# Linear attention with a gated feed-forward block: w3 and w_out loaded and folded first, constants on VectorE, and a newly searched order of steps, loads and queues

## The chip, the cores and the metric

The kernel runs on one core of a Trainium2 chip. The metric is the device time of one execution in microseconds (us). The kernel before takes 258.12 us, the median of three runs (257.49 to 262.9).

Every ratio below is the mean time of one kernel's fast runs over the mean time of the other's fast runs of the same rounds, so it is not quite the ratio of the medians that stand beside it. On one core a run is called slow when it is over 1.5% above the fastest of the same kernel; the others are called fast. Intervals are 95% intervals.

## The reference

There are 8 batches, 8 heads, 576 positions and heads of 64. After the attention the heads of a position are laid side by side, which gives 4608 tokens of 512.

```python
def phi(x):
    return np.where(x > 0, x, np.exp(x) - 1.0) + 1.0
q_p, k_p = phi(q), phi(k)
kv  = np.einsum('bhsd,bhse->bhde', k_p, v)
z   = np.sum(k_p, axis=2)
num = np.einsum('bhsd,bhde->bhse', q_p, kv)
den = np.einsum('bhsd,bhd->bhs', q_p, z)[..., None] + 1e-06
x   = (num / den)          # transposed and reshaped to [4608, 512]
a, b = x @ w1, x @ w2      # [4608, 1024] each
out = ((a * b) @ w3) @ w_out
```

Nothing stands between w3 and w_out, so the kernel multiplies these two matrices once (the fold, `wf = w3 @ w_out`) and uses the product.

## The kernel before

The kernel is a set of small steps and a string of tokens. The string fixes the order in which the steps are written, and so the order of the instructions on each engine: in the traces below every engine and every DMA queue works in that order (ScalarE's copy of 0.39 us that has to wait behind two exponentials is an example). A load that waits for a free buffer holds up everything behind it in its queue.

The tokens that matter here are these. L, M and N load k, q and v of a batch (`.0` and `.1` are halves, `.2` the whole, `.3` the remainder of 64 positions); with a `+` the load goes into GpSimd's queue, without it into SyncE's. X, Y and Z are the exponential, minimum and maximum of q, and x, y and z those of k. T transposes q by a DMA in SyncE's queue, and A forms the products that need it. v copies v to bf16, K forms kv, F is one unit of the two wide products (eight matmuls), O an output product and S its store. E, C and B load w3, w_out and w1 with w2. w and W are the transposes and products of the fold, H runs filler matmuls, and I sets constants.

```python
ld  = ctx.enter_context(tc.tile_pool(name="ld", bufs=5))    # q, k, v: five buffers for all
att = ctx.enter_context(tc.tile_pool(name="att", bufs=2))
...
def load_qkv(name, src, b, part, alt=False):
    ...
    return (nc.gpsimd if alt else nc.sync).dma_start(...)   # "+" picks the queue

def v_unit(b, i, alt=False):                                # token v
    ...
    else:                                                   # v.2, the remainder
        copy_of(alt)(out=vr[:, :, 0:D], in_=raw["vr", b]...)  # VectorE with "+", else ScalarE

def qt_load(b, part):                                       # token T
    qj, qr = ph["q", b]
    ...
    nc.sync.dma_start(out=dst, in_=src, transpose=True)

def nat_units(b, js):                                       # token A: nd <- kv, qt
    ...
    nc.tensor.matmul(nd[...], w[rows], kvs[b][rows, hp, u, :], start=True, stop=True)

def f_unit(c, f):                                           # token F: 8 matmuls, 1.73 us
    a_ps, b_ps = f_open(c, f)
    for ps, w in ((a_ps, w1_sb), (b_ps, w2_sb)):
        for kc in range(KC):
            f_mm(c, f, ps, w, kc)
    f_close(c, f, a_ps, b_ps)                               # ScalarE copies a, VectorE multiplies
...
GATES = "B0<L0.1 C0<N0.1 E4<N0.1 M1.2<C1"                   # load on the left waits for the right
for s in ORDER.split():
    step(s)
```

## Time and profile before

| what | value | where it is from |
|---|---|---|
| time | 258.12 us | median of three runs |
| PE busy | 235.0 us, 92% of the span | first line of the page |
| first useful matmul | 14.79 us | timeline of PE |
| first output product | 58.20 us | timeline of PE |
| from there to the end | 196.7 us | 254.9 us of span less 58.20 |
| longest PE wait after that | 0.9 us, on a transposed q | timeline of PE |

PE is the limit from about 25 us on. Before that, loads and PE compete for being it. The following lines are SyncE's entries in the timeline of the kernel before (start of issue, length of issue, queue, what); they are the transpositions of q of batches 2, 3 and 4.

```profile
66.59 3.31 SPq L242 DMA_TRANSPOSE qt<-qj  x1
...
88.47 1.64 SPq L242 DMA_TRANSPOSE qt<-qj  x1
...
104.55 4.78 SPq L242 DMA_TRANSPOSE qt<-qj  x1
```

PE uses the three results from 76.7, 97.8 and 121.9 us on. They are asked for 10, 9 and 17 us ahead, and they land 8.7, 6.0 and 8.3 us after they are asked for. So the first two have 1 to 3 us to spare, and the third has 9.

### The profile page before, as it was taken

To read this page: it belongs to the slowest core of one execution; us is meant where nothing else is said; L and a number is where in the kernel's file an instruction comes from. 1 tells how busy PE (TensorE), PEld (TensorE's weight loads), DVE (VectorE), ACT (ScalarE), POOL (GpSimd) and SP (SyncE) were. 2 spreads that over 40 slices of the span, in tenths; PEclk is the share of its full clock that TensorE was granted. 3 is DMA by queue.
4 is the path that set the end of the run, shared out by engine and by line. 5 is a ranking of instruction groups with operands and counts; after the bars stand their busy time and mean duration, and the time that the engine had idled before them with its cause. 6 is when DMAs were issued, how large, how long until landed. Compare 5 with 4: busy or idle time off the path is not lost.

```text
span 254.9 us, 4477 instructions
## 1 busy us (share of the span) xinstructions
PE 235.0 (92%) x1641; PEld 114.3 (45%) x1660; DVE 166.9 (65%) x425; ACT 130.4 (51%) x206; POOL 42.7 (17%) x69
## 2 busy tenths in 40 slices
PE   0568999999899999999999999989999999999994
PEld 0134444645454554445445444534454444444442
DVE  0586665659779999897992798668856543333230
ACT  3569526968884674675448337534342213323201
POOL 8784185466100010010000000000000000000000
PEclk9999999999999999999999999999999999999999
DMA  5999999999999999959968946983470331200225
GB/s 186 363 254 202 211 287 231 327 260 337 256 322 219 265 254 280 257 140 255 352 175 221 373 84 165 249 217 24 146 215 3 61 115 53 82 0 0 84 85 165
DMA packets 58726, 49.52 MB, mean 194 GB/s; under 512 B 34448, under 2 KB 49040, under 8 KB 58704
## 3 DMA queue, kind: packets, MB, share of 16 engines
q1 hardware_dynamic: 47344, 26.81, 42.1%
...
q14 instruction: 9, 0.07, 0.2%
q10 hardware_dynamic: 144, 0.13, 0.1%
...
## 4 chain that ended last, share of the span: by engine, by line
PE 74%; DMA 17%; POOL 3%; DVE 2%; issue 1%; ACT 1%; ACTq 0%; SPq 0%; DVEq 0%; POOLq 0%
PE b_ps L371 22%; PE a_ps L371 22%; PE o_ps L390 19%; DMA w_sb<-in_moe_w_dram 4%; PE wf_ps L464 4%; DMA qt<-qj 4%; DMA w3b<-in_moe_w_dram 3%; DMA q32r<-in_q_dram 3%; PE kvp L199 3%; DMA k<-in_k_dram 3%; PE nd L265 2%; PE w3p L454 1%; POOL k L120 1%; PE xtp L285 1%; PE o_ps L417 1%
## 5 line engine op out<-in xcount | busy, mean ns | idle before, releaser
L371 PEld LDWEIGHTS <-w_sb 128*128 128x128 bf16 x576 | 54.5, 98 | 66.5 <-DMA w_sb<-in_moe_w_dram 2.1
L377 DVE TENSOR_TENSOR ab<-a_sb,b_ps 128x512 bf16<-128x512 f32 x72 | 49.2, 685 | 50.7 <-PE b_ps L371 46.5
L371 PE MATMUL b_ps<-xt,w_sb 128*128 128x512 bf16 x288 | 74.9, 379 | 1.2 <-ACT o_sb L393 0.7
L371 PE MATMUL a_ps<-xt,w_sb 128*128 128x512 bf16 x288 | 75.1, 380 | 0.3 <-DMA w_sb<-in_moe_w_dram 0.2
L376 ACT COPY a_sb<-a_ps 128x512 f32<-128x512 f32 x72 | 42.1, 586 | 58.1 <-PE a_ps L371 58.1
L390 PE MATMUL o_ps<-wf_sb,ab 128*128 128x512 bf16 x266 | 63.0, 379 | 0.7
L390 PEld LDWEIGHTS <-ab 128*128 128x128 bf16 x280 | 26.8, 98 | 30.9
L393 ACT COPY o_sb<-o_ps 128x512 f32<-128x512 f32 x22 | 12.8, 585 | 38.5 <-PE o_ps L390 38.4
L162 DVE SCALAR_TENSOR_TENSOR qj<-q,e 128x256 bf16<-128x256 f32 x64 | 23.8, 417 | 0.1
L162 DVE SCALAR_TENSOR_TENSOR kj<-k,e 128x256 bf16<-128x256 f32 x64 | 23.7, 416 | 0.0
L141 DVE TENSOR_SCALAR e<-e 128x1024 bf16<-128x1024 bf16 x32 | 13.7, 430 | 12.6 <-ACT e L137 12.6
L137 ACT ACTIVATE e<-q 128x1024 bf16<-128x1024 f32 x16 | 16.9, 1061 | 6.2 <-DMA q<-in_q_dram 6.2
L137 ACT ACTIVATE e<-k 128x1024 bf16<-128x1024 f32 x16 | 16.8, 1056 | 3.1 <-DMA k<-in_k_dram 2.9
L275 DVE TENSOR_TENSOR xn<-nd,r 128x512 bf16<-128x512 f32 x28 | 18.0, 686 | 0.0
L120 POOL DMA_DIRECT2D v<-in_v_dram x7 | 6.1, 869 | 66.3 <-ACT vt L171 44.1
L464 PE MATMUL wf_ps<-wo_sb,w3t 128*128 128x512 bf16 x60 | 14.6, 379 | 0.3 <-issue 0.2
L100 PE MATMUL warm<-zero 128*128 128x512 bf16 x12 | 4.5, 551 | 9.5 <-DVE zero L94 9.5
L171 ACT CAST vt<-v 128x1024 bf16<-128x1024 f32 x12 | 12.6, 1047 | 0.1
L393 DVE COPY o_sb<-o_ps 128x512 f32<-128x512 f32 x13 | 8.9, 686 | 4.4 <-PE o_ps L390 4.4
L120 POOL DMA_DIRECT2D q<-in_q_dram x7 | 6.1, 875 | 33.3 <-ACT a_sb L376 23.6
L464 PEld LDWEIGHTS <-w3t 128*128 128x128 bf16 x64 | 5.9, 98 | 6.3
L199 PE MATMUL kvp<-vt,kj 64*128 64x130 bf16 x224 | 8.7, 217 | 0.0
...
## 6 DMA issues: line engine op xcount, KB each, us to landing
...
```

The source lines that it names most:

```text
L120: return (nc.gpsimd if alt else nc.sync).dma_start(out=t[:, h0 * W:h1 * W].rearrange("p (h x) -> p h x", x=W), in_=src[b, h0:h1, 0:NJ * P, ...
L137: nc.scalar.activation(out=e, in_=x, func=AF.Exp)
L141: nc.vector.tensor_scalar_min(out=e, in0=e, scalar1=1.0)
L162: nc.vector.scalar_tensor_tensor(out=out, in0=x, scalar=1.0, in1=e, op0=ALU.add, op1=ALU.max)
L199: nc.tensor.matmul(kvp[:, r, i * W:(i + 1) * W], kk[rows], vv[rows], start=(n == 0), stop=(n == (NJ if r == g else NJ - 1)))
L275: nc.vector.tensor_tensor(out=dst.rearrange("p (c u) e -> p u c e", u=2), in0=v4[:, :, :, 0:D], in1=r[0:n].unsqueeze(3).to_broadcast([n, 2 ...
L371: nc.tensor.matmul(ps, w[:, kc, f * P:(f + 1) * P], xt[:, 4 * c:4 * c + 4, kc, :], start=(kc == 0), stop=(kc == KC - 1))
L376: nc.scalar.copy(out=a_sb, in_=a_ps)
L377: nc.vector.tensor_mul(out=abs_[c][:, f, :], in0=a_sb, in1=b_ps)
L390: nc.tensor.matmul(o_ps, ab[:, f, m * P:(m + 1) * P], wf_sb[:, f, :], start=(f == 0), stop=(f == FC - 1))
L393: copy_of(alt)(out=o_sb, in_=o_ps)
L464: nc.tensor.matmul(wfs[i], w3ts[i][:, kc, :], wo_sb[:, kc, :], start=(kc == 0), stop=(kc == FC - 1))
```

## The change

The intent is to give PE work from the start. The fold of w3 and w_out needs no attention and no exponentials, so its loads come first. The loads of the front stand in GpSimd's queue in the order in which they are needed, all but one, as before: until then the remainder of k of batch 0 went through SyncE's queue, now that of v does. GpSimd is freed of six memsets. Then the order of everything was searched anew, and the gates with it.

```diff
         elif part == 1:
-            nc.gpsimd.memset(mask, 0.0)
-            nc.gpsimd.memset(mask[0:D, :, 0, :], 1.0)
...                                            (six in all)
+            nc.vector.memset(mask, 0.0)
+            nc.vector.memset(mask[0:D, :, 0, :], 1.0)
...
     ORDER = """
-    L0.3 M0.0+ X0.0 L0.0+ I1 Y0.0 x0.2 y0.2 M0.1+ Z0.0 x0.0 Z0.1 y0.0 I2 z0.0 z0.4 L0.1+ N0.3+
-    x0.1 H12 N0.0+ N0.1+ X0.1 L1.3+ E0 Y0.1 v0.0 L1.2+ v0.1 z0.1 y0.1 B0 v0.2+ I0 Z0.2 z0.2 Z0.3
-    E1 C0 x1.2 a0.0 B1 b0.0 C1 c0.0 M1.3+ z0.3 d0.0 e0.0 a0.1 e0.1 f0.0 f0.1 B2 E2 c0.1 y1.2 E3
...
+    C0 E0 L0.3+ E1 I2 E2 I0 I1 C1 w0 M0.0+ w1+ w2+ E3 U0 X0.0 M0.1+ L0.0+ X0.1 W0 N0.0+ W1+ x0.0
+    E4 L0.1+ x0.2 Y0.1 E5 Y0.0 W2+ w3 H16 v0.0 M1.3+ Z0.0 N0.3 Z0.1 N1.3+ E6 y0.2 y0.0 x0.1 w4+
+    z0.0 z0.1 N0.1+ y0.1 W3 w5 Z0.2 W4 z0.2 a0.0 E7 b0.0+ Z0.3 z0.4 v0.2 w6 L1.2+ L1.3+ N1.0+
...                                            (batch 1 and the late part, also rewritten)
-    GATES = "B0<L0.1 C0<N0.1 E4<N0.1 M1.2<C1"
+    GATES = "B0<L0.0 L0.0<C1 N1.0<E5"
```

The same steps occur equally often in both strings, but for 16 filler matmuls where there were 12, and the fold product of the fourth row, which was in two pieces (U3 and W3) and is in one. In batches 2 and later, 11 loads have another queue. The transposition of q of batch 4, T4.0, has moved:

```diff
-    O2.2+ S1.1 A3.2 y4.2 P3.3+ T4.0 Y5.0 v4.1 z4.3 x5.0 O2.3+ z4.4 F3.0 F3.1 x5.1 K4.0+ K4.1+
...  (F3.2, F3.3 and O2.1 stand between that line and A4.0)
+    Y5.0 F3.1 x5.2 K4.0+ L7.3 K4.1+ F3.2 M6.3+ Z5.4 T4.0 A4.0 F3.3 L6.2+ x5.1 P3.3+ F3.4 Z5.0
```

More of the change, by code (lines that the diff above doesn't have):

```diff
@@ L85, in constants @@
         elif part == 1:
-            nc.gpsimd.memset(mask, 0.0)
-            nc.gpsimd.memset(mask[0:D, :, 0, :], 1.0)
-            nc.gpsimd.memset(mask[D:P, :, 1, :], 1.0)
-            nc.gpsimd.memset(eps, 1e-6)
-            nc.gpsimd.memset(vt[:, :, :, D:D + 1], 1.0)
-            nc.gpsimd.memset(vr[:, :, D:D + 1], 1.0)
+            nc.vector.memset(mask, 0.0)
+            nc.vector.memset(mask[0:D, :, 0, :], 1.0)
+            nc.vector.memset(mask[D:P, :, 1, :], 1.0)
+            nc.vector.memset(eps, 1e-6)
+            nc.vector.memset(vt[:, :, :, D:D + 1], 1.0)
+            nc.vector.memset(vr[:, :, D:D + 1], 1.0)
         else:
@@ L470 @@
     ORDER = """
-    L0.3 M0.0+ X0.0 L0.0+ I1 Y0.0 x0.2 y0.2 M0.1+ Z0.0 x0.0 Z0.1 y0.0 I2 z0.0 z0.4 L0.1+ N0.3+
-    x0.1 H12 N0.0+ N0.1+ X0.1 L1.3+ E0 Y0.1 v0.0 L1.2+ v0.1 z0.1 y0.1 B0 v0.2+ I0 Z0.2 z0.2 Z0.3
-    E1 C0 x1.2 a0.0 B1 b0.0 C1 c0.0 M1.3+ z0.3 d0.0 e0.0 a0.1 e0.1 f0.0 f0.1 B2 E2 c0.1 y1.2 E3
-    b0.1+ M1.2+ w0 d0.1 g0.0 e0.2 e0.3 f0.2 g0.1 B3 h0.0 f0.3 E4 x1.0 g0.2 z1.4 h0.1 h0.2 g0.3
-    h0.3 i0.0 y1.0 i0.1 x1.1 w1 z1.0 F0.2 X1.2 z1.1 N1.3+ y1.1 F0.3 U0 z1.2 W0+ F0.4 E5 M2.3+
-    F0.5 Y1.2 X1.0 w2+ E6 Y1.0 Z1.0 N1.0+ w3 W1 W2+ X1.1 F0.6 U3 Z1.1 E7 N1.1+ Y1.1 w4 M2.2+
@@ L477 @@
-    Z1.2 W3 v1.0+ a1.0 Z1.3 b1.0 w5 F0.7 X2.2 Y2.2 Z1.4 z1.3 w6 W4 w7 L2.2+ a1.1 v1.1+ b1.1 W5+
-    v1.2 K1.0+ L3.3+ K1.1+ L2.3+ W6 X2.0 X2.1 A1.0 Y2.0 Z2.0 x2.0 W7 N2.3+ x2.1 x2.2 A1.1 T1.1
-    P1.1 O0.0 O0.1 Y2.1 Z2.4 N2.2+ P1.0 L3.2+ y2.2 y2.0 Z2.1 M0.3+ O0.3 z2.0 y2.1 v2.1 P1.2 Z2.2
-    P1.3+ v2.0 z2.1 z2.2 X0.2 Z2.3 Y0.2 z2.4 v2.2+ A1.2 x3.0 T2.0 z2.3 O0.2 M3.3+ S0.3 F1.0 x3.2
-    M3.2+ F1.1 X3.0 Y3.0 K2.0+ y3.0 K2.1+ N3.3 X3.1 F1.2 S0.1 M4.3 F1.3 Z0.4 z3.0 x3.1 y3.2 N3.2
-    z3.4 X3.2 F1.4 A2.0 Y3.1 F1.5 M4.2+ T0.1 F1.6 A2.1 P2.1 L4.3 v3.2+ F1.7 Z3.0 Y3.2 D1.1 Z3.1
@@ L483 @@
-    S0.0 Z3.2 O1.0 y3.1 P2.2+ X4.2 L4.2 z3.1 r0 Z3.3 v3.1 O1.1+ N4.3 v3.0+ P2.0 X4.0 z3.2 O1.3
-    F2.0 T2.1 N5.3 z3.3 T3.0 N4.2+ Z3.4 K3.0+ X4.1 A2.2 Y4.0 Y4.2 F2.1 P2.3 K3.1+ Z4.0 x4.0 y4.0
-    F2.2 M5.3 Y4.1 O1.2 z4.0 Z4.4 A3.0 F2.3 L6.3 Z4.1 L5.3 x4.2 Z4.2 F2.4 M5.2 x4.1 P3.0+ S0.2
-    T3.1 P3.1 z4.1 Z4.3 F2.5 F2.6 A3.1 X5.0 F2.7 v4.2+ v4.0 y4.1 X5.2 L5.2 P3.2 z4.2 X5.1 S1.0
-    O2.2+ S1.1 A3.2 y4.2 P3.3+ T4.0 Y5.0 v4.1 z4.3 x5.0 O2.3+ z4.4 F3.0 F3.1 x5.1 K4.0+ K4.1+
-    y5.0 Y5.2 z5.0 Z5.4 S1.3 Z5.0 M6.3 x5.2 T4.1 F3.2 F3.3 Z5.1 D3.1 z5.1 O2.1 Y5.1 A4.0 S1.2
@@ L489 @@
-    x6.2 L7.3 Z5.2 F3.4 N5.2 F3.5 S2.3 D2.1 L6.2 v5.1 y5.1 A4.1 z5.2 M6.2+ F3.6 D4.0 y6.2 F3.7
-    X6.0 S2.2 z5.3 v5.0+ O2.0 S2.1 O3.0 Z5.3 x6.0 x6.1 O3.2 M7.3 y5.2 T5.0 L7.2 z5.4 Y6.0 O3.3
-    v5.2+ y6.0 F4.0 X6.1 X6.2 K5.0+ Y6.2 K5.1+ F4.1 Y6.1 F4.2 z6.0 F4.3 M7.2 Z6.0 N6.2 A5.0 Z6.4
-    F4.4 Z6.1 F4.5 A5.1 Z6.2 O3.1 N6.3 F4.6 T5.1 z6.4 F4.7 y6.1 v6.1 S2.0 D5.0 S3.0 v6.2 z6.1
-    z6.2 X7.0 O4.0+ Z6.3 Y7.0 x7.0 y7.0 O4.1+ S3.2 x7.2 T6.0 v6.0 O4.3 A4.2 z6.3 K6.0+ D4.1 F5.0
-    F5.1 A5.2 X7.1 K6.1+ F5.2 N7.2+ A6.0 T6.1 S3.3 Z7.0 F5.3 X7.2 F5.4 S3.1 D5.1 Y7.1 F5.5 A6.1
@@ L495 @@
-    Z7.1 O4.2+ N7.3 y7.2 v7.0 S4.1 A6.2 F5.6 x7.1 F5.7 Z7.2 y7.1 Z7.3 O5.0+ z7.4 Y7.2 S4.0 D6.0
-    S4.3 Z7.4 z7.0 S5.0 O5.1 v7.1 z7.1 O5.2+ F6.0 v7.2 z7.2 T7.1 O5.3 z7.3 K7.0+ K7.1+ F6.1 F6.2
-    F6.3 T7.0 S4.2 S5.3 A7.0 F6.4 F6.5 A7.1 F6.6 F6.7 S5.1 D7.0 O6.2+ A7.2 O6.3+ O6.0 F7.0 F7.1
-    S6.3 D7.1 S5.2 S6.0 F7.2 F7.3 F7.4 O6.1 F7.5 F7.6 F7.7 D6.1 F8.0 F8.1 S6.1 O7.1 S6.2 F8.2
-    F8.3 F8.4 F8.5 O7.3 F8.6 F8.7 S7.3 O7.0+ O8.0+ S7.1 O7.2+ S7.0 O8.1 O8.3 S7.2 S8.1 S8.0 S8.3
-    Q8.2
+    C0 E0 L0.3+ E1 I2 E2 I0 I1 C1 w0 M0.0+ w1+ w2+ E3 U0 X0.0 M0.1+ L0.0+ X0.1 W0 N0.0+ W1+ x0.0
@@ new lines @@
+    E4 L0.1+ x0.2 Y0.1 E5 Y0.0 W2+ w3 H16 v0.0 M1.3+ Z0.0 N0.3 Z0.1 N1.3+ E6 y0.2 y0.0 x0.1 w4+
+    z0.0 z0.1 N0.1+ y0.1 W3 w5 Z0.2 W4 z0.2 a0.0 E7 b0.0+ Z0.3 z0.4 v0.2 w6 L1.2+ L1.3+ N1.0+
+    z0.3 W5 N2.3+ w7+ c0.0 N1.1+ a0.1 d0.0 B0 b0.1+ X1.2 e0.0 v0.1 x1.0 f0.0 x1.2 x1.1 c0.1 y1.0
+    W6 z1.0 g0.0 d0.1 Y1.2 e0.1 z1.1 e0.2 Z1.4 f0.1 e0.3 f0.2 v1.0+ M1.2+ g0.1 M2.3+ W7+ y1.1
+    v1.1 B1 f0.3 g0.2 B2 h0.0 X1.0 y1.2 h0.1 h0.2 z1.2 X1.1 g0.3 M2.2+ z1.4 Y1.0 B3 z1.3 h0.3
+    Z1.0 Y1.1 v1.2 i0.0 Z1.1 i0.1 K1.0+ L2.2+ Z1.2 K1.1+ F0.2 F0.3 a1.0 X2.2 Z1.3 b1.0 F0.4 a1.1
@@ new lines @@
+    X2.0 b1.1+ Y2.0 Z2.0 X2.1 Y2.1 F0.5 A1.0 F0.6 L2.3+ F0.7 A1.1 x2.0 P1.0 L4.3+ Z2.1 O0.3+
+    Y2.2 S0.3 x2.1 x2.2 P1.1 y2.2 N2.2+ T1.1 M0.3+ L3.2 Z2.2 O0.1+ Z2.4 M3.3 Z2.3 y2.0 y2.1
+    v2.1+ P1.2 z2.0 N4.3 P1.3 O0.2+ v2.0 z2.1 N3.3 X0.2 z2.4 O0.0 F1.0 M3.2+ Y0.2 z2.2 X3.0 z2.3
+    X3.1 T2.0 A1.2 v2.2+ F1.1 X3.2 F1.2 Y3.0 K2.0+ K2.1+ Z3.0 F1.3 Z3.1 L3.3+ A2.0 N3.2+ x3.0
+    F1.4 Z0.4 F1.5 T0.1 L4.2 x3.1 y3.0 P2.1 A2.1 F1.6 v3.2+ M4.3 D1.1 Y3.1 F1.7 z3.0 v3.0 S0.1
+    M4.2+ Y3.2 Z3.4 P2.0 X4.0 x3.2 v3.1 y3.2 Y4.0 P2.2 O1.1+ Z3.2 S0.0 x4.2 Z3.3 r0 z3.4 X4.1
@@ new lines @@
+    y3.1 z3.1 O1.3 P2.3+ z3.2 O1.2 z3.3 F2.0 F2.1 x4.0 S0.2 K3.0+ K3.1+ Y4.1 X4.2 N4.2+ F2.2
+    x4.1 T3.0 L5.3 A3.0 F2.3 y4.0 Z4.0 y4.1 y4.2 v4.2 z4.4 Y4.2 P3.0 Z4.1 S1.2 F2.4 M7.3+ F2.5
+    T2.1 z4.0 T3.1 O1.0 Z4.4 P3.1 A3.1 F2.6 M5.3 Z4.2 S1.1 M5.2 P3.2 z4.1 Z4.3 L5.2 T4.1 F2.7
+    N5.3 X5.0 X5.2 A2.2 z4.2 v4.1+ v4.0+ A3.2 O2.3 z4.3 F3.0 X5.1 x5.0 O2.1 S1.0 Y5.2 S1.3 N5.2+
+    Y5.0 F3.1 x5.2 K4.0+ L7.3 K4.1+ F3.2 M6.3+ Z5.4 T4.0 A4.0 F3.3 L6.2+ x5.1 P3.3+ F3.4 Z5.0
+    A4.1 Y5.1 F3.5 y5.1 D4.0 M6.2+ F3.6 y5.2 Z5.1 y5.0 D3.1 z5.0 F3.7 Z5.2 Z5.3 D2.1 S2.3 z5.1
@@ new lines @@
+    X6.2 v5.0 z5.4 O2.2 N7.3 T5.0 Y6.2 O3.3+ z5.2 x6.0 Z6.4 x6.1 v5.2 S2.2 O2.0+ S2.0 y6.1 v5.1
+    A4.2 K5.0+ O3.0+ S2.1 X6.0 N6.3+ F4.0 z5.3 F4.1 K5.1+ x7.2 F4.2 S3.3 A5.0 F4.3 M7.2 L6.3+
+    X6.1 Y6.1 Y6.0 Z6.0 O3.2+ A5.1 Z6.1 x6.2 y6.0 y6.2 F4.4 z6.4 y7.2 F4.5 z7.4 O3.1 N6.2+ v6.2+
+    v6.0 Z6.2 z6.0 T5.1 z6.1 Z6.3 F4.6 D5.0 F4.7 K6.0+ X7.0 A5.2 S3.2 O4.2+ F5.0 S3.0 S3.1 v6.1+
+    z6.2 F5.1 z6.3 F5.2 X7.2 X7.1 Y7.2 O4.0+ L7.2 K6.1+ Z7.4 T6.0 D4.1 Y7.0 F5.3 Z7.0 x7.0 x7.1
+    A6.0 F5.4 N7.2+ O4.3 v7.2 S4.0 v7.0 A6.1 F5.5 F5.6 D5.1 y7.0 S4.2 Z7.1 F5.7 Y7.1 y7.1 z7.0
@@ L501 @@
+    S4.3 O4.1 O5.3 D6.0 v7.1+ Z7.2 Z7.3 z7.1 F6.0 z7.2 O5.0 O5.2+ z7.3 S4.1 S5.3 F6.1 T7.0 K7.0+
+    K7.1+ F6.2 A7.0 F6.3 T7.1 O5.1 F6.4 T6.1 A7.1 D7.0 F6.5 F6.6 S5.1 F6.7 O6.1 O6.3+ F7.0 A7.2
+    A6.2 F7.1 S6.3 F7.2 F7.3 S6.1 F7.4 F7.5 D7.1 S5.2 D6.1 S5.0 O6.2+ F7.6 S6.2 O6.0+ F7.7 F8.0
+    F8.1 F8.2 S6.0 F8.3 F8.4 F8.5 F8.6 F8.7 O7.3+ O8.0 O8.3+ O8.1+ S7.3 O7.1+ S8.0 S8.3 O7.0+
+    S8.1 O7.2 S7.0 S7.1 S7.2 Q8.2
     """
-    GATES = "B0<L0.1 C0<N0.1 E4<N0.1 M1.2<C1"
+    GATES = "B0<L0.0 L0.0<C1 N1.0<E5"
```

## The prediction

> **What bounds the kernel now.** I read the page first (slices, then the chain that ended last), then the PE timeline of the first 70 us, the stretches of 2 us with their DMA rates, and the waits of DVE and ACT on loads. From the page:
>
> ```profile
> PE 235.0 (92%) x1641; PEld 114.3 (45%) x1660; DVE 166.9 (65%) x425; ACT 130.4 (51%) x206; POOL 42.7 (17%) x69
> ...
> PE   0568999999899999999999999989999999999994
> ...
> PEclk9999999999999999999999999999999999999999
> DMA  5999999999999999959968946983470331200225
> ...
> PE 74%; DMA 17%; POOL 3%; DVE 2%; issue 1%; ACT 1%; ACTq 0%; SPq 0%; DVEq 0%; POOLq 0%
> ```
>
> A slice is 6.4 us. PE is full from the fourth slice to the end, and DMA is full in the second to the seventeenth. So there are two stages: a front in which loads and PE compete for being the limit, and then some 190 us of PE. Only the front can give anything. Its PE timeline (start, duration, what, idle before it):
>
> ```profile
> 9.47 4.47 PE L100 MATMUL warm<-zero 128*128 128x512 bf16 x12 [9.47 <-DVE zero L94]
> 14.79 0.61 PE L309 MATMUL tp<-ident,qj 128*128 128x128 bf16 x8 [0.86 <-POOL ident masks.py:199]
> ...
> 17.96 0.39 PE L330 MATMUL den<-qt,kvz 128*128 128x512 bf16 x1 [1.68 <-DVE kvz L320]
> ...
> 58.20 3.42 PE L390 MATMUL o_ps<-wf_sb,ab 128*128 128x512 bf16 x15
> ```
>
> The first useful matmul is at 14.79 us. At 58.20 us the first output product begins: by then chunk 0 of the two wide products and the whole fold of w3 and w_out are done. I use that point as a milestone, because the data needed up to there are nearly the same in both kernels.
>
> PE's work I count in issue slots, since the modelled ends overlap: in the chain eight 512-column matmuls take 1.73 us (0.216 each), eight transposes 0.45 us (0.056 each), a batch's 36 kvp matmuls 1.13 us. Up to 58.20 us: fold 64 x 0.056 + 64 x 0.216 = 17.4; attention of batch 0 by 16 transposes, 20 kvp and 8 wide matmuls 0.9 + 1.6 + 1.7 = 4.2; chunk 0 64 x 0.216 = 13.8; of batch 1 16 transposes, kvp, two nd groups of 16 at 0.35 and four transposes 0.9 + 1.1 + 0.7 + 0.2 = 2.9. Sum 38.3, so 58.2 - 38.3 = 19.9 us of the front were not useful work. The chain ends PE's work at 251.05 us, and 3.85 us of copy and store follow.
>
> The loads, stretch by stretch (columns: length, busy time of each engine, clock, DMA share, GB/s):
>
> ```profile
> 4.00:6.00 2.00, 0.00 (x0) 0.00 (x0) 0.00 (x0) 0.29 (x1) 2.00 (x5) 1.00 1.02 381
> 6.00:8.00 2.00, 0.00 (x0) 0.00 (x0) 1.20 (x5) 1.94 (x3) 2.00 (x4) 1.00 1.00 371
> ...
> 24.00:26.00 2.00, 1.97 (x10) 0.83 (x9) 1.04 (x3) 1.76 (x3) 0.25 (x2) 1.00 1.41 197
> ```
>
> The rate counts bytes as they land. Weights land as bf16 from float32, so 197 GB/s of them is 394 GB/s read: by bytes read the rate hardly depends on the kind of load. Two waits date the stream:
>
> ```profile
> 50.65 0.70 DVE L171 CAST vt<-v 128x1024 bf16<-128x1024 f32 x1 [0.32 <-DMA v<-in_v_dram]
> ...
> 23.37 10.43 DMA w_sb<-in_moe_w_dram
> ```
>
> Before the second half of v of batch 1 (awaited until 50.65) the kernel had asked for all weights (w3 4.19 MB, w_out 2.10, w1 and w2 4.19), q, k, v of two batches (6.29) and six remainders of 0.13: 17.6 MB. The third quarter of w2, landed at 33.80, had 11.0 MB up to it. The first q half (0.52 MB plus a remainder on the other queue) was awaited until 5.71. A line "landed at 3.9 us + bytes / 0.376 MB per us" gives 50.7, 33.2 and 5.6: good within a microsecond.
>
> **What the Trainium skill says.** "DMA: Bandwidth & Descriptors", section "Issuing engines are not separate DMA queues": transfers started by any engine run on the same 16 DMA engines, and several issuers save issue time only. The full DMA slices agree with that reading, so moving loads to one queue makes no bandwidth; it fixes an order. Its section "Bandwidth" measures 341 GB/s for 1 MB and 425 for 16 MB; this trace's 371 to 394 lie between, and I use the trace. "TensorE: Matmul & The Clock Gate", section "What's actually happening": PE runs at half clock until about 3.4 us of sustained work. The trace agrees: the warm-up matmuls begin 0.43 us apart (weight loads at 9.88, 10.30, 10.73) and speed up after 12.86, 3.4 us after the first.
>
> **The change, part by part.**
>
> Constants: six memsets leave GpSimd (2.89 to about 4.07 us, 1.2 us of its queue) for VectorE, which did nothing until 6.80 us. The DMA engines already had 1.2 MB queued then, over 3 us of work. Worth 0 on the path.
>
> PE work: I counted the order's steps. Every product, transpose and store occurs equally often, and only the dummy matmuls go from 12 to 16. The work left after the milestone is the same. The drains of some products move from ACT to DVE, which has room (65%).
>
> Loads: the new queue begins w_out half, w3 row, k remainder, two w3 rows, the other w_out half, q half, w3 row, q half, k half, v half, w3, k half, w3, two remainders, w3, v half, w3; then k and v of batch 1 with remainders, the first quarter of w1 and w2, q of batch 1, the second and third quarter, q of batch 2, the last quarter. With the line fitted above:
> - first w3 row at 1.6 MB: 8.1 us, so useful PE work starts near 8 instead of 14.8, at half clock.
> - second half of w_out at 3.9 MB: 14.4. Fold rows 0 to 2 end near 19.
> - the fifth w3 row at 7.1 MB: 22.8. Here stand the 16 dummies, 3.5 us if warm: the search put filler just where PE has no data.
> - last w3 row at 10.0 MB: 30.4. PE keeps up; the rest of batch 0's attention mixed with fold rows 6 and 7 takes about 7 us, to 38.
> - first quarter of w1, w2 at 13.4 MB: 39.5. Second at 15.6: 45.4. Last at 18.75: 53.8.
>
> From 45.4 PE does four of chunk 0's eight units (8 matmuls each), two sets of transposes and an nd group: 2 x 1.73 + 0.45 + 1.73 + 0.45 + 1.73 + 0.35 = 8.2, to 53.6; waits for the last quarter to 53.8; and does the last two units in 3.45, to 57.2. Work done there: 17.4 + 4.2 + 13.8 + 1.1 + 0.9 + 0.35 = 37.8. Not useful: 57.2 - 37.8 = 19.4, against 19.9 before. So the 7 us gained at the start are spent again by waits for w1 and w2, which now come after more bytes. Gain of the front 0.5 us.
>
> After the milestone the trace of before shows two PE waits above half a microsecond, 0.9 on a transposed q (at 167.8) and 0.7 on ACT's o_sb copy (at 69.3). A new order may lose them or make others; I credit half, 0.8. Sum 1.3 us off 258.1: about 256.8.
>
> **Rivals.**
>
> (A) The intent comes true: PE starts 6.7 us earlier and keeps it. For it: PE's first two slices are nearly empty. Against it: DMA is full there, and 18.75 MB have to land before chunk 0 ends. If loads came at the best observed 0.394, the last quarter would be there at 51.5, 2.3 us earlier: 254.5. The whole gain would be 251.4.
>
> (B) One in-order queue stalls. The load of v of batch 1 reuses the buffer of q of batch 0, which DVE frees only after a copy that waits for PE near 29 us, by my reckoning at about 30. At that time k of batch 1 (1.05 MB, 2.8 us) is still to move, so I expect no empty DMA. If PE or DVE were 4 us later than I think, w1 and w2 would slip by 2 to 3 us: 260.
>
> (C) PE stays at half clock in the front, as it works in pieces of 0.5 us between loads. 24 fold matmuls and 16 dummies at 0.43 instead of 0.216 cost 8.6 us, but PE then still reaches the second quarter not much after 45.4: 0 to 2 us, 258.
>
> (D) The late order meets a wait on a DMA transpose or a full PSUM buffer that the old one had not: 1 to 3 us, 258 to 260.
>
> **Range and chances.** The load line is good to 1 us in before, the reckoning of PE's pieces to perhaps 2, the late waits to 2, and the median of the three runs to 0.5 (257.49 to 262.9). Together about 3 us either way, a little wider for order effects: 252.8 to 260.3. Faster by over 2% needs 252.96 or less, that is most of (A): 0.12. Slower by over 2% needs 263.3, (B) and (D) together: 0.07. Within 2%: 0.81.
>
> **What would show it.** Right: PE's first w3p near 8 us; DMA full from the second slice on; weight loads of PE waiting on w_sb between 38 and 54 us, several microseconds in sum; the first o_ps after chunk 0 near 57 us; from there to the end 197 us as before. Wrong: o_ps beginning at or before 54 (loads faster, or needed fewer bytes), a DMA slice below 9 in the first eight (the queue stalled), or a stage after the milestone that is 2 us shorter or longer than before's 196.7.

## The result, and the profile after

The changed kernel takes 276.38 us (three runs: 275.89, 276.38 and a slow one of 280.27). The ratio to the kernel before is 1.0711 (1.0641 to 1.0781): it is 7% slower. The predicted 256.8 us was 19.6 us too low, and the result lies far outside the range of 252.8 to 260.3.

These are the lines of the page after that answer to those of before, from a fast run. A slice is now 6.85 us.

```profile
PE 243.9 (89%) x1664; PEld 117.1 (43%) x1664; DVE 175.0 (64%) x440; ACT 123.0 (45%) x197; POOL 50.9 (19%) x74
...
PE   0499986999967997999299999999999999999994
...
PEclk9999999799997999999869999999999999999999
DMA  6999999996891699799924795994760053120044
...
PE 69%; DMA 25%; POOL 3%; issue 1%; ACT 1%; POOLq 0%; ACTq 0%
```

PE does its first work in the second slice, as intended. But there are new holes in PE's row: a 6 in the seventh slice, still in the front, a 6 and a 7 in the twelfth and thirteenth, a 7 in the sixteenth, and a 2 in the twentieth. The clock row has digits below 9, and the DMA row falls to 1 and 2 in the slices beside these holes. In the chain, DMA has grown from 17% to 25%; the same part of the page puts 12% of the span down to the transposed q.

The front, from the timeline of PE after (start, length, what, idle before it):

```profile
9.60 1.03 PE L454 MATMUL w3p<-ident,w3b 128*128 128x128 bf16 x8 [9.60 <-DMA w3b<-in_moe_w_dram]
...
48.33 0.21 PE L199 MATMUL kvp<-vr,kr 64*128 64x130 bf16 x1 [2.47 <-ACT vr L176]
...
49.24 1.65 PE L371 MATMUL a_ps<-xt,w_sb 128*128 128x512 bf16 x4
50.68 1.91 PE L371 MATMUL b_ps<-xt,w_sb 128*128 128x512 bf16 x4
...
63.33 1.89 PE L390 MATMUL o_ps<-wf_sb,ab 128*128 128x512 bf16 x8
```

The first fold matmuls begin at 9.60 us. The first output product begins at 63.33 us, 5.1 us later than before. The timeline of ScalarE says what the 2.47 us wait was for:

```profile
45.98 2.00 ACT L137 ACTIVATE e<-q 128x1024 bf16<-128x1024 f32 x2 [2.25 <-DMA q<-in_q_dram]
47.89 0.39 ACT L176 CAST vr<-v32r 128x256 bf16<-128x256 f32 x1
```

The copy of v's remainder of batch 1 takes 0.39 us, and its data had long been there. It stands behind two exponentials of q of batch 1, and these waited for a load that landed at 45.96. Directly after this pause the groups of four matmuls take 1.65 and 1.91 us where they normally take 1.03 (the granted clock from 48 to 52 us is 0.69 on average).

The larger loss comes later. From 63.33 us to the end of the span of 273.9 us are 210.6 us, against 196.7 before: 13.9 us more. The timeline of PE, in the stretch from 80 to 145 us:

```profile
83.94 0.62 PE L265 MATMUL nd<-kv,qt 64*128 64x65 bf16 x16 [4.38 <-DMA qt<-qj]
84.50 1.89 PE L371 MATMUL a_ps<-xt,w_sb 128*128 128x512 bf16 x4
...
107.65 0.42 PE L265 MATMUL nd<-kv,qt 64*128 64x65 bf16 x16 [1.64 <-DMA qt<-qj]
...
135.55 0.62 PE L265 MATMUL nd<-kv,qt 64*128 64x65 bf16 x16 [5.54 <-DMA qt<-qj]
136.10 1.89 PE L371 MATMUL a_ps<-xt,w_sb 128*128 128x512 bf16 x4
```

PE waits three times for a transposed q: 4.38 + 1.64 + 5.54 = 11.6 us. After the two long waits it runs slowly. From 83.94 to 87.49 it took 3.55 us for work that normally takes 2.1; from 135.55 to 142.62 it took 7.1 us for work of 4.0 (the same steps from 107.65 to 111.69). Together that is some 4.5 us. Waits and slow clock make 16.1; the kernel before had 1.6 us of waits here, so these account for 14.5 us, where 13.9 were lost.

The same three transpositions in SyncE's queue after:

```profile
73.67 5.65 SPq L242 DMA_TRANSPOSE qt<-qj  x1
...
98.56 1.32 SPq L242 DMA_TRANSPOSE qt<-qj  x1
...
120.89 7.47 SPq L242 DMA_TRANSPOSE qt<-qj  x1
```

They are asked for 7, 10 and 16 us later than before (5.1 of that is the later first output product), and they land 10.2, 9.0 and 14.6 us after that (83.90, 107.61 and 135.50). The waits end 0.04 to 0.05 us after these landings. The DMA engines were not simply overloaded all along. These stretches of 10 us, first of the kernel before, show the busy time of PE, its weight loads, DVE, ACT and POOL, then clock, DMA share and GB/s:

```profile
80.00:90.00 10.00, 9.95 (x77) 5.04 (x76) 9.82 (x29) 6.46 (x12) 1.04 (x1) 1.00 1.19 208
...
130.00:140.00 10.00, 9.95 (x78) 4.89 (x77) 5.01 (x14) 6.98 (x12) 0.00 (x0) 1.00 0.94 235
```

and then of the changed kernel:

```profile
80.00:90.00 10.00, 6.06 (x53) 2.98 (x54) 5.21 (x14) 2.31 (x5) 0.00 (x0) 0.83 0.36 126
...
130.00:140.00 10.00, 4.46 (x30) 2.17 (x30) 2.98 (x9) 1.54 (x2) 1.23 (x2) 0.74 0.96 262
```

From 80 to 90 us the DMA share is 0.36, and from 130 to 140 us it is 0.96 while PE does less than half of its work. Stretches of 4 us tell more about the first: from 80 to 84 us, while PE waits for the transposition, the share is still 0.89, and from 84 to 92 us it is 0.02 and 0.14. So this hole comes after the late transposition. VectorE too had waited 5.23 us for it, until 84.02, because its next maximum writes the buffer that the transposition reads, and between 75.61 and 88.81 us neither queue asked for anything. GpSimd's queue shows the burst of the second stretch:

```profile
97.20 0.88 POOL L120 DMA_DIRECT2D v<-in_v_dram  x1 [20.70 <-ACT vt L171]
121.07 0.90 POOL L120 DMA_DIRECT2D v<-in_v_dram  x1 [21.75 <-ACT er L137]
124.39 0.90 POOL L120 DMA_DIRECT2D k<-in_k_dram  x1 [0.79 <-DVE r L273]
126.69 0.89 POOL L120 DMA_DIRECT2D q<-in_q_dram  x1 [1.40 <-DVE er L141]
```

Twice the queue stood still for over 20 us, by the profile until ScalarE had done what the next load of v waited for. These pauses alone are not the difference: in the kernel before the same queue stood still for 21.03 us until 88.96 and for 23.60 us until 113.70. The difference is what comes beside T4.0. In the changed kernel GpSimd asks for v, k and q within 6 us from 121 us on, just after SyncE has asked for T4.0 (120.89); in the kernel before it asks for nothing between the issue of T4.0 (104.55) and its landing (112.9).

### The profile page after: what moved, and what is told of

It is laid out like the page before. It is cut to its first block, busy times and chain, and to the rows that moved or that the text cites. A ratio compares the mean times of both kernels' runs of the same rounds, so it can differ in the third digit from the quotient of the medians.

```text
span 273.9 us, 4508 instructions
## 1 busy us (share of the span) xinstructions
PE 243.9 (89%) x1664; PEld 117.1 (43%) x1664; DVE 175.0 (64%) x440; ACT 123.0 (45%) x197; POOL 50.9 (19%) x74
## 4 chain that ended last, share of the span: by engine, by line
PE 69%; DMA 25%; POOL 3%; issue 1%; ACT 1%; POOLq 0%; ACTq 0%
PE a_ps L371 21%; PE o_ps L390 21%; PE b_ps L371 20%; DMA qt<-qj 12%; DMA q<-in_q_dram 4%; DMA wo_sb<-in_moe_w_out_dram 3%; DMA w3b<-in_moe_w_dram 3%; DMA k32r<-in_k_dram 3%; PE nd L265 3%; PE kvp L199 2%; PE xtp L285 1%; POOL w3b L445 1%; PE o_ps L417 1%; POOL k L120 1%; ACT e L137 0%
## 5 line engine op out<-in xcount | busy, mean ns | idle before, releaser
L371 PE MATMUL a_ps<-xt,w_sb 128*128 128x512 bf16 x288 | 78.6, 394 | 0.0
L371 PE MATMUL b_ps<-xt,w_sb 128*128 128x512 bf16 x288 | 77.2, 388 | 0.4 <-DMA w_sb<-in_moe_w_dram 0.4
L120 POOL DMA_DIRECT2D v<-in_v_dram x10 | 8.4, 840 | 90.0 <-ACT vt L171 41.9
L393 ACT COPY o_sb<-o_ps 128x512 f32<-128x512 f32 x16 | 9.3, 585 | 30.2 <-PE o_ps L390 30.1
L393 DVE COPY o_sb<-o_ps 128x512 f32<-128x512 f32 x19 | 13.1, 688 | 14.6 <-PE o_ps L390 14.6
L265 PE MATMUL nd<-kv,qt 64*128 64x65 bf16 x224 | 6.3, 198 | 11.6 <-DMA qt<-qj 11.6
L454 PE MATMUL w3p<-ident,w3b 128*128 128x128 bf16 x64 | 6.2, 254 | 11.0 <-DMA w3b<-in_moe_w_dram 10.8
L265 PEld LDWEIGHTS <-qt 64*128 64x128 bf16 x224 | 4.5, 99 | 17.1 <-DMA qt<-qj 13.0
L455 DVE COPY w3t<-w3p 128x1024 bf16<-128x1024 bf16 x4 | 2.8, 692 | 12.6 <-PE w3p L454 12.6
L171 ACT CAST vt<-v 128x1024 bf16<-128x1024 f32 x10 | 10.5, 1047 | 0.0
```

Of the source, the lines that this page charges most:

```text
L120: return (nc.gpsimd if alt else nc.sync).dma_start(out=t[:, h0 * W:h1 * W].rearrange("p (h x) -> p h x", x=W), in_=src[b, h0:h1, 0:NJ * P, ...
L265: nc.tensor.matmul(nd[0:n, u, hp * (D + 1):(hp + 1) * (D + 1)], w[rows], kvs[b][rows, hp, u, :], start=True, stop=True)
L371: nc.tensor.matmul(ps, w[:, kc, f * P:(f + 1) * P], xt[:, 4 * c:4 * c + 4, kc, :], start=(kc == 0), stop=(kc == KC - 1))
L393: copy_of(alt)(out=o_sb, in_=o_ps)
```

## The experiments

Fifteen kernels were run, all with correct results. Each edit moves or re-flags tokens of one of the two strings, or joins parts of both. The kernel before was run beside them each time; its medians were 257.67 us (e1 to e4), 257.68 (e5 to e9), 258.57 (e10 to e12), 260.03 (e13 to e15) and 257.0 (e16).

| run | what | median us | range | ratio of fast runs (interval) |
|---|---|---|---|---|
| e1 | after, three transpositions early, loads behind them | 287.58 | 285.28 to 289.98 | 1.114 (1.105 to 1.123) |
| e2 | new front, old late part | 258.92 | 257.42 to 260.37 | 1.0052 (0.9986 to 1.0118) |
| e3 | old front, new late part | 290.71 | 284.54 to 294.06 | only one run fast |
| e4 | after, v's remainder first | 291.61 | 274.8 to 300.53 | only one run fast |
| e5 | after, k of batch 3 on GpSimd | 281.82 | 280.38 to 290.35 | 1.0918 (1.0863 to 1.0973) |
| e6 | after, first store behind T2.0 | 275.82 | 271.83 to 283.57 | 1.060 (1.053 to 1.067) |
| e7 | after, old queues late | 269.02 | 266.19 to 272.48 | 1.0355 (1.031 to 1.040) |
| e9 | e2, v's remainder first | 257.68 | 256.89 to 261.37 | 0.9994 (0.996 to 1.0028) |
| e10 | e7, T4.0 early | 261.66 | 260.58 to 267.59 | 1.014 (0.9999 to 1.028) |
| e11 | before, new queues late | 263.22 | 258.45 to 268.25 | 1.003 (0.9903 to 1.0158) |
| e12 | before, T4.0 late | 259.28 | 257.66 to 259.98 | 1.0046 (0.9954 to 1.0137) |
| e13 | e10, v's remainder first | 262.60 | 261.23 to 268.0 | 1.0124 (1.0046 to 1.0202) |
| e14 | after, two loads behind T4.0 | 266.62 | 265.93 to 279.72 | 1.0288 (1.0213 to 1.0363) |
| e15 | e9, a fold row earlier | 256.31 | 254.74 to 257.69 | 0.9895 (0.9805 to 0.9986) |
| e16 | e15, more of the fold earlier | 255.31 | 254.65 to 256.61 | 0.9964 (0.9911 to 1.0017) |

There is no e8: by the author's account a kernel with six or seven buffers for q, k and v instead of five could not be built, for lack of room; no run shows this. So whether more buffers would cure the changed order stays open.

### e1: the three transpositions early, in the changed kernel

The first theory was that only the places of the transpositions in SyncE's queue are wrong.

```diff
+ Z2.3 T2.0 L3.2 M3.3 ...      (T2.0 directly behind the last write of its input, the loads behind it)
+ Z3.3 T3.0 ...
+ Z4.3 T4.0 M5.2 ...
```

> The changed kernel with three DMA transposes of q (batches 2, 3, 4) put on SyncE's queue right after the last write of their input, ahead of the loads that stood before them; nothing else moved. Theory (late transposes): PE's waits on qt, 11.6 us in the changed kernel, fall below 2 us, the drops of the granted clock at 84 and 136 us go (about 4 us), time 276.4 -> 262 (260 to 265). Rival (the transposes are slow because the DMA engines are full whatever the order): waits on qt stay above 7 us, time 270 or more.

It took 287.58 us, so this theory fell. The longest wait on a transposed q was now 2.9 us, but PE stood still for other reasons. Its two longest waits, from its timeline:

```profile
83.05 0.85 PE L265 MATMUL nd<-kv,qt 64*128 64x65 bf16 x16 [7.55 <-DVE kv L204]
...
141.47 1.87 PE L371 MATMUL a_ps<-xt,w_sb 128*128 128x512 bf16 x4 [15.40 <-ACT o_sb L393]
```

The second one waited for ScalarE to empty an output from PSUM. ScalarE had been idle for 19.41 us at an exponential of q of batch 5, whose load was asked for at 123.1 and landed at 139.6. A transposition that waits for its input holds up the loads behind it; a late load holds up ScalarE; ScalarE's copies stand behind its exponentials, and PE stops for want of a free PSUM buffer. The queues are linked, and a place that is too early does as much harm as one that is too late.

### e2 and e3: front and late part exchanged

Both kernels change strings after F0.7, the last unit of the first chunk. The rest is what is left to do, in the order of the other string; in e3 that includes the last rows of the fold and a part of batch 1, which the old front had not done by then.

```diff
e2: - ... F0.7 <rest of the new string>     + ... F0.7 <rest of the old string, old queues>
e3: - ... F0.7 <rest of the old string>     + ... F0.7 <rest of the new string, new queues>
```

> The changed kernel's order up to the end of chunk 0, then what is left in the order of the kernel before. Theory (two separate losses: 5 us in the front, 14 us late, the late one made by the late order): first output product still near 63 us, from there to the end 197 us, time 262 (260 to 264). Rival (the late waits follow from the front's lateness, by loads that come later): late stage stays over 205 us, time 270 or more.

> The order of the kernel before up to the end of chunk 0, then what is left in the changed kernel's order (GpSimd constants, old gates). Theory (the late order makes the late loss on its own): waits of PE on qt of 6 to 12 us, time 266 to 272. Rival (the late order is harmless when the front is on time): waits on qt under 3 us, time 256 to 260.

The new front with the old late part takes 258.92 us, ratio 1.0052: the interval includes no difference. The old front with the new late part takes 284.54 us in its only fast run. So the late part makes the loss, after either front, though for the old front this rests on one fast run. Why e3 is even worse than the changed kernel is open: its late part also holds the unfinished steps of the front, and its profile is of a slow run.

### e4: the copy of v's remainder first

```diff
- ... h0.0 X1.0 ... Y1.1 v1.2 i0.0 ...
+ ... h0.0 v1.2 X1.0 ... Y1.1 i0.0 ...
```

> The changed kernel with ScalarE's small copy of v's remainder of batch 1 moved ahead of the two exponentials of q of batch 1. Theory: PE's wait of 2.5 us at 45.5 us (kvp on ScalarE's vr) goes and with it the drop of the clock at 48 to 53 us (2 us); the first output product moves from 63.3 to 59 to 60 us; time 276.4 -> 272 to 274, less if the late waits grow by as much. Rival (w1 and w2 not there yet, the loads are the bound): PE waits for w_sb instead, first output product at 62 us or later, time within 1 us of 276.4.

The wait on ScalarE's copy was gone from the profile, and the first output product came at 58.44 us. The time was hardly better: 274.8 us in the only fast run, and up to 300.53. In the profile the wait for q of batch 2 had grown from 4.38 to 10.03 us. In this run the late part took up what the front gave (214.4 us from the first output product on, instead of 210.6), so the front's own worth cannot be read in this kernel.

### e5 and e6: what stands before the first transposition

In the changed kernel k of batch 3 is loaded by SyncE, behind the first store of an output. That store waits until 66.5 us for its data. Before, GpSimd asked for this load at 58 us; now SyncE asks at 69.

```diff
e5: - L3.2 ... M3.3          + L3.2+ ... M3.3+             (GpSimd's queue)
e6: - Y2.2 S0.3 x2.1 ...     + Y2.2 x2.1 ... T2.0 S0.3     (the store behind the transposition)
```

> The changed kernel with two loads of batch 3 (k, and the remainder of q) issued by GpSimd as before, not by SyncE; same order. The first theory (place of the transposes) fell with the run that moved them and was slower. Second theory: in SyncE's in-order queue these loads stand behind the store of the first output, which waits for the product at 65 us, so k of batch 3 is asked for at 69 us in place of 55, the DMA engines run dry near 65 us, and all later loads bunch up. It expects k of batch 3 to be asked for before 60 us, the first PE wait on qt (4.4 us at 84 us) to shrink below 1.5 us, time 276.4 -> 262 to 267. Rival (the order of the late steps itself asks too late, whatever the queue): time 271 or more, with waits near 130 us as before.

> The changed kernel with the first output store moved on SyncE's queue behind the transpose of q of batch 2; all loads stay on the queues they have. Second theory (the store blocks the loads behind it): k of batch 3 is asked for by 60 us though it is still SyncE that asks; time 262 to 267, like the run with the loads on GpSimd. Rival: 271 or more.

Both repairs brought the load forward. In e5 it was asked for at 60 us, in e6 at 46. In e6 the first wait for a transposed q was gone; in e5 it was 2.94 us, where less than 1.5 was expected. The loss came back later: in e5 the wait for q of batch 4 was 9.45 us, in e6 7.66. The times are 281.82 and 275.82 us; the ratio of e6, 1.060, is not clearly below that of the changed kernel, as the intervals overlap. Repairing the first wait does not repair the kernel.

### e7: the old queues for the late loads

```diff
- L3.2  M3.3  N3.2+ L4.3+ L6.3+ M6.3+ N5.2+ L6.2+ M7.3+ N6.2+ N6.3+
+ L3.2+ M3.3+ N3.2  L4.3  L6.3  M6.3  N5.2  L6.2  M7.3  N6.2  N6.3     (each in its own place)
```

> The changed kernel with every load of batches 2 to 7 on the queue (GpSimd or SyncE) that it had in the kernel before; the order of steps stays the new one. 13 loads change their queue, two of them in the front's list (they belong to batches 2 and later). If the queues are all of the late loss: 260 to 264. If only the two loads of batch 3 matter: the same as the run with those two, within 3 us. If the order of the late steps is what costs: 270 or more.

It took 269.02 us, ratio 1.0355 after 1.0711. So about half of the loss, some 9 us, went with the queues of 11 loads (the expectation counts 13; the two of batch 0 were not moved). Not all of it need be theirs: in the profile the first output product comes at 59.77 us, 3.6 us sooner than in the changed kernel, with the same front. What is left shows in this profile, which fell in a slow run (272.48 us), as one long wait:

```profile
130.38 0.62 PE L265 MATMUL nd<-kv,qt 64*128 64x65 bf16 x16 [10.89 <-DMA qt<-qj]
```

This is T4.0. Its input was written by 109.99 us (the expectation of e10 below says 111.5, which is the date of k's last write), it was asked for at 115.91 behind v of batch 5 and the remainders of k and q, and it landed at 130.33.

### e9: the new front, mended, with the old late part

```diff
  e2, and  - ... h0.0 X1.0 ... v1.2 i0.0     + ... h0.0 v1.2 X1.0 ... i0.0
```

> New front, old late order (258.9 us in its own run), with ScalarE's copy of v's remainder of batch 1 ahead of the exponentials of q of batch 1. Theory: the PE wait on ScalarE's vr near 45 us (1.6 us there) and the clock drop after it go, so the first output product comes 2 to 4 us sooner: 255 to 257, which would be faster than before. Rival (w1 and w2 land too late for it to help): 258 to 259.

It took 257.68 us, ratio 0.9994: above the 255 to 257 of the theory. The first output product came at 60.22 us instead of 62.05. The new front, with the old late part behind it and the copy in its place, is worth just as much as the old front. The gain against e2 (0.6%) has the size of the wait that was taken away, 1.59 us in the profile of e2, but the intervals overlap.

### e10, e11 and e12: the two parts of the late loss, together and alone

e10 is e7 with T4.0 moved ahead of v of batch 5. e11 and e12 put each defect by itself into the kernel before.

```diff
e10: - ... L5.2 T4.1 F2.7 N5.3 ... N5.2 ... T4.0 A4.0     + ... L5.2 T4.1 T4.0 F2.7 N5.3 ... N5.2 ... A4.0
e11: the old string, with the 11 flags of the new one
e12: - ... P3.3+ T4.0 Y5.0 ... O2.1 Y5.1 A4.0             + ... P3.3+ Y5.0 ... O2.1 Y5.1 T4.0 A4.0
```

> The changed order with the old queues for the loads of batches 2 and later (the run that took 269), and one thing more: the transposition of q of batch 4 (T4.0) goes to directly behind T4.1 in SyncE's queue, ahead of v of batch 5 and three small loads. In the 269 us run its input was written at 111.5, it was asked for at 115.9 and landed at 130.3, behind 2 MB of v and q; PE waited 10.9 us for it and ran at half clock afterwards. Theory (the two parts of the late loss are the queues, about 7 us, and the place of this one transposition, about 10): it is asked for near 110 to 112, lands before 120, PE's wait for it is gone, and the time is 257 to 261. Rival (the late order as a whole is tighter, and something else will take the place of this wait): 265 to 270, with a new PE wait of 5 us or more at another place.

> The kernel before in its own order, with nothing changed but the queue of the 11 late loads that the change moved between SyncE and GpSimd. Theory (the queues by themselves cost some 7 us, as giving them back took 7 us off the changed kernel): 263 to 267, with PE waits for a transposed q. Rival (the old order has the slack to stand them; queues cost only together with the new order): 257 to 260.

> The kernel before, with one token moved: the transposition of q of batch 4 goes from its place before F3.0 to directly before the products that need it (A4.0), as the change has it. It is then asked for behind seven other entries of SyncE's queue, some 14 us later than at 104.55, near 119, and lands near 126, while PE needs it at 122. Theory: a PE wait of 4 to 7 us on the transposed q there, slower clock for 3 us after it, time 262 to 267. Rival (PE has other work to run, or the queue does not hold it up): 257 to 259.

e10 took 261.66 us, just above the range of the theory. The long wait was gone, and no other of its size took its place. In SyncE's queue, then on PE (from a fast run):

```profile
110.37 4.21 SPq L242 DMA_TRANSPOSE qt<-qj  x1
```

```profile
119.76 0.42 PE L265 MATMUL nd<-kv,qt 64*128 64x65 bf16 x16
```

T4.0 is asked for 5.5 us earlier, lands after 6.3 us instead of 14.4, and PE goes on without a wait. The ratio falls from 1.0355 to 1.014 with this one token.

What is left in this fast profile has the same shape. The transposition of q of batch 6 was asked for at 156.30 us, half a microsecond before GpSimd asked for v, and it landed after 14.7 us. PE waited for it:

```profile
171.09 0.42 PE L265 MATMUL nd<-kv,qt 64*128 64x65 bf16 x16 [2.43 <-DMA qt<-qj]
```

Behind this wait PE was slow again, by some 1.6 us (171.44 to 176.69 us for 16 matmuls that normally take 3.46, with 0.2 of idle time). The span is 4.2 us longer than that of the kernel before: 1.8 us up to the first output product (59.97 us) and 2.4 us after it, which this wait and the slow clock more than cover.

e12 came out near the rival: 259.28 us, and at most 1.4% above the kernel before by its interval. T4.0 was asked for at 114.92, 10 us later than in the kernel before, and landed at 122.41; PE used it at 123.93. The old order had 9 us to spare there and kept 1.5 of them. e11 is not clear. Two runs took 258.45 and 258.85 us, two took 267.59 and 268.25, and only the first two count as fast, so by the fast runs the queues cost nothing that can be seen in the old order (the interval leaves room for 4 us). The profile is of one of the long runs, and in it T4.0 took 18.4 us from issue to landing, yet PE waited only 1.06 us for it. The granted clock of that run, 0.999, is not lower than in the fast ones, so what made two runs long stays open. The theory that T4.0 costs 10 us wherever it stands fell with e12. That the queues cost 7 us wherever they stand is not seen in the fast runs, but two of four runs were as long as it said, so e11 does not settle it.

### e13: does the last part close the sum?

```diff
  e10, and  - ... h0.0 X1.0 ... v1.2 i0.0     + ... h0.0 v1.2 X1.0 ... i0.0
```

> The run before that took 261.7 (changed order, old queues late, transposition of q of batch 4 ahead) with one thing more: ScalarE's copy of v's remainder of batch 1 stands ahead of the exponentials of q of batch 1. Theory (what was left is the front's wait, 0.9 us in that run's profile and 2.5 in the changed kernel's, plus the slower clock after it): 258 to 260.5, within 1% of the kernel before, so that three named repairs make up the whole loss of 18 us. Rival (something unnamed in the late order costs the rest): still 261 to 263.

The rival was right: 262.6 us, ratio 1.0124, no better than e10 within the intervals. In the front of e10 the copy cost only 0.9 us. The larger part of what was left is the wait for q of batch 6, which e10's profile shows and which no run repaired. The profile of e13 fell in its slow run (268.0 us) and is not compared.

### e14: why the transposition took so long to land

The changed kernel keeps its order and queues, but for two loads of 1 MB that GpSimd asked for at the same moment as T4.0.

```diff
- ... N5.2+ ... M6.3+ Z5.4 T4.0 A4.0 F3.3 L6.2+ ...
+ ... M6.3+ Z5.4 T4.0 N5.2 L6.2 A4.0 F3.3 ...
```

> The changed kernel in its own order and queues, but for two loads: v and k of batch 5 and 6 go from GpSimd's queue to SyncE's, directly behind the transposition of q of batch 4 instead of beside it. Theory (the transposition was slow because its transfer shared the DMA engines with those loads): it lands within 9 us of being asked for (14.6 before), PE's wait of 5.5 us near 135 is gone or under 1.5, and the time is 267 to 271. Rival (the transposition is slow by itself, or late because its input is late): it again takes 12 us or more, and the time is 274 to 278.

It took 266.62 us, ratio 1.0288, a little better than expected. SyncE's queue, from a fast run:

```profile
120.42 2.93 SPq L242 DMA_TRANSPOSE qt<-qj  x1
123.45 0.53 SPq L120 DMA_DIRECT2D v<-in_v_dram  x1
```

T4.0 is asked for at the same time as in the changed kernel (120.42 against 120.89), and it lands after 5.0 us instead of 14.6, at 125.46. PE's wait of 5.5 us is gone. The transposition is not slow by itself, and its input was not the cause: it was slow beside loads whose later arrival made no new wait in this run. The edit changes both the moment and the queue of these loads (v is now asked for at 123.45, by SyncE), so which of the two counts is not shown. That they share the DMA engines agrees with what the Trainium skill says in "DMA: Bandwidth & Descriptors", section "Issuing engines are not separate DMA queues": the transfers of all issuers interleave on the same 16 engines. This one edit, with the first wait of 4.25 us still in the profile, took 4% off the changed kernel. A part of that is chance: of the 8.8 us between the two profiled spans, 3.3 lie before the first output product (60.08 us instead of 63.33), where the two kernels have the same order, and 5.5 after it.

### e15 and e16: can the gain of the front be had?

These start from e9, which ties with the kernel before, and attack the filler matmuls and waits of PE between 19 and 27 us.

```diff
e15: - E3 U0 X0.0 M0.1+ ... E4 ... w3 H16 ... w4+ ... W3 w5      + E3 U0 X0.0 E4 M0.1+ ... w3 w4+ W3 H8 ... w5
     - L1.2+ L1.3+ N1.0+ ... B0                                  + L1.2+ L1.3+ B0 N1.0+ ...
e16: - W1+ x0.0 L0.1+ x0.2 Y0.1 E5 Y0.0 W2+ w3 w4+ W3 H8 ... w5 Z0.2 W4
     + W1+ w3+ x0.0 L0.1+ x0.2 W2+ w4+ Y0.1 E5 Y0.0 W3 W4 H4 ... w5 Z0.2
```

> New front, v's remainder first, old late order (the run that took 257.7), with three small edits in the front: the fifth row of w3 is loaded before the second half of q instead of four loads later, its transposes and products run before the filler matmuls, of which 8 stay instead of 16, and the first quarter of w1 and w2 is loaded before v of batch 1. Theory (the intent of the change is sound, PE's filler and waits between 19 and 24 us can be replaced by 2.2 us of fold work): 255 to 257, ratio to before 0.990 to 0.997. Rival (the first stage of attention, which sets when the wide products start, is not earlier, and PE waits there instead): 257.5 to 259.

> The run that took 256.3 (new front mended, old late order), with the fourth row's copy of transposed w3 on VectorE and put ahead of the exponentials, the fourth row's transposes before the third row's products, and the fifth row's products before the filler, of which 4 matmuls stay. Theory (PE is busy without a break from 26.6 us on, so what is taken out before that moves the end): the wait of 2.3 us on the copy and about 1.4 us of half clock after it go, time 253 to 255, ratio to before 0.98 to 0.987. Rival (attention of batch 0 is not ready earlier, and PE waits there instead): 255.5 to 257, ratio 0.988 to 0.995, with new PE waits between 30 and 42 us.

e15 took 256.31 us, ratio 0.9895 (0.9805 to 0.9986). That is a gain as the theory had it, though the kernel before was slower than usual in those rounds (260.03 us), so the size is uncertain. PE's timeline shows one long wait left in the front:

```profile
23.43 3.34 PE L464 MATMUL wf_ps<-wo_sb,w3t 128*128 128x512 bf16 x8 [2.30 <-ACT w3t L455]
```

Again it is a copy of ScalarE behind exponentials, and again the matmuls after it run at half speed: 3.34 us for eight, where 1.89 is normal. e16 moved that copy to VectorE and took 255.31 us in six fast runs between 254.65 and 256.61; the kernel before had 257.0 in the same rounds. The theory had 253 to 255. By the ratio, 0.9964 (0.9911 to 1.0017), it is not told apart from the kernel before. The first output product came at 57.59 us, against 59.54 in e15. But a part of the wait came back one row later, as this line shows, and PE waited another 0.82 us for the attention of batch 0 near 36 us, as the rival had it:

```profile
27.41 0.61 PE L454 MATMUL w3p<-ident,w3b 128*128 128x128 bf16 x8 [1.64 <-ACT w3t L455]
```

So the front can be improved by some tenths of a per cent to 1%, and not by the 7 us of the earlier start. No version beat the kernel before clearly.

## Why the prediction was wrong

**The bound and the milestone** were read rightly, but for trifles (the fourth slice of PE reads 8, not 9). The new front with the old late part ties with the kernel before (e2 at 1.0052, and e9, with a copy mended, at 0.9994), near the gain of 0.5 us that the sum gave the front. That the sum came so near is in part luck, as its parts were off. One premise was wrong without harm to the sum: no loads were "moved to one queue". SyncE's queue holds one entry before 49 us in the kernel before, and one before 66 us in the changed one. So the full DMA slices of the front come from one issuer, and they do not test what the Trainium skill says about several.

**Constants, filler and dates of loads.** The memsets were worth nothing, as far as the profile goes: PE's first wait after the change is for a load of w3, not for a constant. This was not run by itself. The load line was 1 to 3.5 us early: first w3 row at 9.6 instead of 8.1, the last at 31.6 instead of 30.4, the first quarter of w1 and w2 at 41.9 instead of 39.5, the last at 57.4 instead of 53.8. PE still waited only 0.44 us for w1 and w2, where the prediction had set "several microseconds", because it was late itself: it came to the wide products at 41.16 us instead of 38, and after 45.86 a wait for ScalarE hid the load. The second quarter landed at 47.6 (w1) and 48.8 us (w2); without the wait for ScalarE PE would have been ready for it near 46.6 (an estimate: 45.46 plus 1.13 for the products for kv). So the late loads would have taken back a part of what repairing that wait gives.

**The step of the front that failed** is "From 45.4 PE does four of chunk 0's eight units ... to 57.2". PE was there at 45.46, by luck: not because the second quarter had landed, but because it had begun two units when the first one landed, at 41.98. But the products for kv of batch 1, 1.13 us, also stand behind that point, and they had been counted only in the sum of the work, not in this stretch. And the reckoning followed only PE and the loads, not ScalarE's order. The copy of v's remainder stood behind the exponentials of q: 2.47 us of wait and about 1.7 of slow clock (16 matmuls from 49.24 to 54.39, 5.15 us where 3.46 is normal). With another 0.6 for a product and transposes that the new order puts before the milestone, 57.2 + 0.6 + 1.1 + 2.5 + 1.7 = 63.1, and the trace has 63.33. This loss is not constant, and the changed kernel's profile has the latest milestone: five fast profiles of kernels with the same order up to there (e1, e2, e5, e10, e14) have the milestone between 59.27 and 62.05 us and this wait between 0.2 and 1.59 us. In e14 the load of q landed 1.6 us earlier. Two fast profiles of the old front have 58.20 and 59.31 us (before, e12), so the new front is usually 1 to 4 us late, and 5.1 in the run compared here.

**The step that failed most** is "The work left after the milestone is the same", and with it "A new order may lose them or make others; I credit half, 0.8". The count of the work was right and said nothing about its time: 210.6 us instead of 196.7. What has to be compared there is, for each transfer that PE needs, how far ahead it is asked for, and what else is asked for at that moment. The prediction looked at neither. The flags of 11 late loads and the place of T4.0 could be read in the two strings beforehand.

**Rival (D)** named the mechanism, "a wait on a DMA transpose", and gave it 1 to 3 us. Only the size was off: three waits of 11.6 us in all and 4.5 us of slow clock after them. **Rival (B)**, a stall of an in-order queue, did not come in the front as it was drawn: v of batch 1 was asked for at 31.25 us, near the expected 30, and the DMA slices two to nine are full. In the late part GpSimd's queue stands still for over 20 us twice, but it does so in the kernel before too. (A) fell with e2, and (C) is visible in the fold's first matmuls (1.03 us for eight transposes, where 0.61 is normal) but the filler matmuls from 20.02 us on, at normal speed, show that PE had time to spare then.

**What the runs put in its place.** The ratio falls from 1.071 to 1.036 with the old queues (e7), to 1.014 with T4.0 ahead of the loads (e10). The 1.2 to 1.4% that remain are, in e10's profile, a front that is 1.8 us later and the wait of 2.43 us for q of batch 6 with its slow clock; moving the copy of v's remainder does not take them away (e13), and no run repaired that wait. How the sizes divide between queues and front is blurred by the 3 us by which the same front varies from profile to profile. The place of T4.0 costs little in the old order (e12), and the queues cost nothing clear (e11): there the transposition of batch 4 has 9 us to spare, in the new order with the new queues it is asked for 9 us ahead and takes 14.6. The loss is thus one of lost slack: a transposition that is asked for late meets a burst of loads and lands late (e14 shows this for batch 4; for batches 2, 3 and 6 it is argued from their like). What stays open is which of the 11 loads makes the first transposition late: moving the one that looked most guilty, k of batch 3, did not repair the kernel (e5, e6). Also open is how far more buffers would help.

## What to carry to other kernels

Equal counts of work do not make equal times when every queue is in order: for each transfer on the critical engine's path, compare the time from its issue to its use with the time it takes to land, in the kernel before and in the changed string, and look at what the other queues ask for in the same moment. A copy that empties PSUM or feeds PE should not stand behind work that waits for a load, on the same engine. After repairing one wait, look for the next one before believing the gain: of six repairs of the changed kernel (e1, e4, e5, e6, e7, e14), only two (e7, e14) made it clearly faster. And compare a suspect pause with the kernel before: GpSimd's pauses of over 20 us stand in both.

## What the Trainium skill lacked or had wrong

- "DMA: Bandwidth & Descriptors", section "Issuing engines are not separate DMA queues", calls the time to initiate a DMA "usually small relative to the DMA itself". For a transposition in SyncE's queue this did not hold: the issue took from 1.17 us (the remainder of q) to 7.47 us (T4.0, half of the 14.6 us to its landing), and whatever stood behind it in the queue waited for that long.
- The same page, section "DMA Transpose (X-bar)", gives constraints, and the page elsewhere a bandwidth, but neither gives a time to landing beside other transfers. Here a transposition took 2.3 us to land with little else in flight (remainder of q, asked for at 88.81 in the changed kernel), 6.0 to 8.7 us for the three of the kernel before that are shown above, 14.6 in a burst, and 18.4 in a long run of e11.
- "TensorE: Matmul & The Clock Gate", section "What's actually happening", lets the clock fall after an idle window of about 3.4 us. Here shorter pauses were followed by half speed (2.47 us in the changed kernel: 1.65 and 1.91 us for four matmuls; 2.30 us in e15: 3.34 for eight), while a pause of 2.91 us in e1 was not (1.04 for the next four). The length of one pause does not decide it.
